# Windowed attention, low-rank mixer and MLP: all engines in one planned order, the mixer per head pair, exp then mask, and the mixer term added inside PSUM

## The chip, the cores and the metric

The kernel runs on one core of one Trainium2 chip. The metric is the device time of one execution in microseconds (us), median over several runs; lower is better. A profile is one execution recorded by the hardware profiler; its span runs from the first to the last instruction. PE is the matmul of TensorE, PEld its weight load, DVE is VectorE, ACT ScalarE, POOL GpSimd. "Fast" and "slow" are the two states that runs are sorted into; only fast runs are compared.

## The reference, cut to what matters

```python
# q, k, v: (4 batches, 8 heads, 768 positions, 64) in fp32; 8 global keys, a window of 96 keys
scores = q @ k.T / 8 - slope[h] * dist          # dist: distance, or 96 for a global key out of the window
scores = where(is_global | is_local, scores, -1e9)
a = softmax(scores);  x = a @ v                  # x: (4, 768, 512) after joining the heads
h = (x.T @ U @ V).T                              # U: (768, 32), V: (32, 768): mixes positions
u = x + h
out = u + relu(u @ w_ch1) @ w_ch2                # 512 -> 2048 -> 512
```

## The kernel before

Positions come in six blocks of 128, so a query block needs its own key block, the one before it, and the 8 global keys. Keys lie on the partitions of the score tiles. The parts that the argument touches:

```python
# loads: one transfer for each head, and for q, k and v; source runs of 64 fp32 = 256 B
nc.gpsimd.dma_start(stg[:, :, hi], src[b, h0 + hi].rearrange("(n p) d -> p n d", p=P))

# scores of a head: VectorE scales them out of PSUM and adds the bias, ScalarE takes exp
nc.vector.scalar_tensor_tensor(out=sprime[hi][:, soff:soff + tot], in0=sc[:, 0:tot],
    scalar=isl, in1=relcat[:, soff:soff + tot], op0=ALU.mult, op1=ALU.add)
nc.scalar.activation(epT[hi][:, 0:GOFF], sprime[hi], AF.Exp, scale=slope[h])

def mixer(b):                                    # a whole batch at once
    nc.scalar.activation(x16, xb, AF.Copy)       # 128 x 3072
    ... tmp = U.T x (6 matmuls of N=512), then for each of 6 token blocks:
        nc.tensor.matmul(h_ps, v16w[:, st * P:(st + 1) * P], tmp16, start=True, stop=True)
        nc.vector.tensor_tensor(xb[:, st], xb[:, st], h_ps, ALU.add)
    ... 24 transposes of fp32 x+h on TensorE, 8 copies to fp16 uT

# MLP in chunks of 512 tokens, held as a queue of small jobs
nc.tensor.matmul(hps, w1_16[:, dc, jt * P:(jt + 1) * P], uT[:, dc, tslice], ...)   # N=512
nc.scalar.activation(htr[:, jt], hps, AF.Relu)
nc.tensor.matmul(cps, htr[:, jc, tt * P:(tt + 1) * P], w2_16[:, jc], ...)           # N=512
nc.vector.tensor_tensor(osb, cps, x_sb[:, n], ALU.add)

for i, (b, hp) in enumerate(pairs):              # the order, by hand
    attention_pair(b, hp, loads.pop(0), fill)    # fill() puts MLP jobs between attention steps
    ...
    fill(3)
    if hp == 0 and b >= 1:
        mixer(b - 1)                             # after the first pair of the next batch
        ...
```

The softmax here doesn't subtract the row's maximum and nothing guards it: scores larger than these inputs give would overflow.

## Time and profile before

| | before |
|---|---|
| time, median of 4 runs | 339.56 us (338.38 to 340.17) |
| span of the profiled run | 341.3 us |
| first hidden-layer matmul (`hps`) starts | 74.2 us |
| TensorE idle from there to its end at 337.4 us | 263.2 - 244.0 = 19.2 us |

The first lines of the profile page. The first line gives busy time, share of the span and number of instructions for each engine; the rows below show the busy tenths of 40 slices of the span (PEclk: the granted clock of TensorE; DMA: the 16 DMA engines).

```profile
PE 288.9 (85%) x1808; PEld 137.7 (40%) x1808; DVE 148.9 (44%) x328; ACT 128.7 (38%) x165; POOL 93.7 (27%) x128
...
PE   0576745899879997998889899968999999999995
...
PEclk9999999999996999899999989998999999999999
DMA  6999999817991932386993307300200020011011
...
DMA packets 82452, 20.31 MB, mean 59 GB/s; under 512 B 76768, under 2 KB 78848, under 8 KB 82432
```

The same by stage. Columns of each row: the stretch and its length, busy time and instructions of each engine, granted clock, DMA share, GB/s.

```profile
core 0: us, PE busy (x) PEld busy (x) DVE busy (x) ACT busy (x) POOL busy (x), PEclk, DMA share, GB/s
0.00:74.20 74.20, 44.89 (x317) 24.71 (x318) 40.76 (x108) 23.02 (x22) 49.42 (x74) 1.00 1.25 114
74.20:240.00 165.80, 146.60 (x1038) 68.86 (x1037) 89.61 (x191) 77.03 (x95) 44.32 (x54) 0.95 0.55 47
240.00:341.30 101.30, 97.36 (x456) 44.12 (x454) 18.54 (x30) 28.68 (x48) 0.00 (x0) 1.00 0.10 39
```

TensorE is the bound in the third stage and nearly so in the second; in the first, 22% of the time, it is busy 60% and waits for others. Part of what it waits for at the end of that stage is the mixer of batch 0. The chain of waits between 54 and 75 us (start, length, what) shows it as one line of dependent work, 18.5 us from the cast to the first hidden-layer matmul:

```profile
55.78 2.77 ACT x_703 L262
...
58.59 2.73 PE tmp_ps L266 x6
...
62.08 0.58 PE h_ps L275
...
67.94 1.31 PE tpu L285 x5
...
70.05 4.27 PE tpu L285 x19
74.33 0.86 PE hps L307 x4
```

The groups of TensorE instructions (count | busy us, mean ns of one). A mean is no spacing, because the records of successive matmuls overlap: the mean is 386 ns, but the last 64 hidden-layer matmuls took 13.81 us by the chain of waits, which is 216 ns each.

```profile
L307 PE MATMUL hps<-uT,w_16_135 128*128 128x512 f16 x384 | 96.7, 386 | 0.3 <-DVE qT_1888 L186 0.3
L319 PE MATMUL cps<-w_16_136,htr 128*128 128x512 f16 x384 | 87.4, 382 | 0.1
...
L285 PE MATMUL tpu<-ident,x_sb 128*128 128x128 f32 x96 | 18.8, 360 | 1.9 <-DVE x_sb L278 1.8
```

### The profile page before, as it was taken

Reading aid. Unit: us, or ns where it says so; the run is one execution under the profiler, and the core shown is the slowest. Engines: PE = TensorE matmul, PEld = TensorE weight load, DVE = VectorE, ACT = ScalarE, POOL = GpSimd, SP = SyncE. Lnnn points to the kernel's source line nnn. Section 1 sums busy time; section 2 is a strip of 40 time slices with the busy share of each in tenths; the row PEclk is TensorE's granted clock in tenths of the full one; section 3 lists DMA queues with packets and bytes.
Section 4 is the critical chain, followed back from the end, with each engine's and each line's share of the span. In section 5 each row is a group of like instructions: output and inputs, shape, how many; then the busy total and the mean of one; then the engine's idle time right before and its main releaser. Section 6 shows DMA issues by size and latency. Waiting matters only on the chain.

```text
span 341.3 us, 4492 instructions
## 1 busy us (share of the span) xinstructions
PE 288.9 (85%) x1808; PEld 137.7 (40%) x1808; DVE 148.9 (44%) x328; ACT 128.7 (38%) x165; POOL 93.7 (27%) x128
## 2 busy tenths in 40 slices
PE   0576745899879997998889899968999999999995
PEld 0244322373333343643344363334354444444442
DVE  3564835565653537755553485662290010020011
ACT  1044444215456610276464016665006305504700
POOL 9966867204452310342350003100000000000000
PEclk9999999999996999899999989998999999999999
DMA  6999999817991932386993307300200020011011
GB/s 41 117 131 144 121 178 138 115 7 48 69 70 11 92 74 43 23 56 40 69 71 73 73 2 46 25 1 2 92 0 31 2 92 31 2 61 62 2 61 61
DMA packets 82452, 20.31 MB, mean 59 GB/s; under 512 B 76768, under 2 KB 78848, under 8 KB 82432
## 3 DMA queue, kind: packets, MB, share of 16 engines
q0 software_dynamic: 78976, 13.74, 51.6%
q1 hardware_dynamic: 3456, 6.29, 4.8%
q8 instruction: 14, 0.23, 0.3%
q14 instruction: 6, 0.05, 0.1%
HBM read 27.46 MB, written 6.29 MB: 99 GB/s over the span
## 4 chain that ended last, share of the span: by engine, by line
PE 66%; DVE 13%; ACT 8%; issue 7%; POOL 4%; DMA 1%; DVEq 0%; ACTq 0%; POOLq 0%
PE cps L319 25%; PE hps L307 21%; PE tpu L285 5%; PE sc L217 5%; PE ob L249 4%; DVE x_sb L278 2%; DVE x_sb L257 2%; POOL qkst L156 2%; PE tmp_ps L266 2%; PE tp L178 2%; PE sc L205 1%; PE h_ps L275 1%; DMA qkst<-in_k_dram 1%; ACT x_703 L262 1%; DVE rcp L254 1%
## 5 line engine op out<-in xcount | busy, mean ns | idle before, releaser
L311 ACT ACTIVATE htr<-hps 128x512 f16<-128x512 f32 x96 | 56.6, 597 | 147.7 <-PE hps L307 147.7
L307 PE MATMUL hps<-uT,w_16_135 128*128 128x512 f16 x384 | 96.7, 386 | 0.3 <-DVE qT_1888 L186 0.3
L319 PE MATMUL cps<-w_16_136,htr 128*128 128x512 f16 x384 | 87.4, 382 | 0.1
L319 PEld LDWEIGHTS <-htr 128*128 128x128 f16 x384 | 36.8, 98 | 48.2 <-issue 7.1
L324 DVE TENSOR_TENSOR osb<-cps,x_sb 128x512 f32<-128x512 f32 x24 | 16.6, 691 | 89.5 <-PE cps L319 89.3
L307 PEld LDWEIGHTS <-w_16_135 128*128 128x128 f16 x384 | 33.6, 98 | 42.7 <-issue 12.2
L156 POOL DMA_DIRECT2D qkst<-in_q_dram x32 | 26.8, 852 | 74.4 <-PE tp L178 74.0
L178 PE MATMUL tp<-ident_93,qkst 128*128 128x128 f16 x192 | 18.8, 249 | 12.9 <-DMA qkst<-in_q_dram 10.2
L156 POOL DMA_DIRECT2D qkst<-in_k_dram x32 | 28.0, 894 | 0.0
L178 PEld LDWEIGHTS <-qkst 128*128 128x128 f16 x192 | 14.4, 111 | 20.1 <-issue 14.2
L285 PE MATMUL tpu<-ident,x_sb 128*128 128x128 f32 x96 | 18.8, 360 | 1.9 <-DVE x_sb L278 1.8
L285 PEld LDWEIGHTS tpu<-ident,x_sb 128*128 128x128 f32 x96 | 15.5, 188 | 7.8 <-DVE x_sb L278 4.4
L257 DVE TENSOR_TENSOR x_sb<-ob,rcp 128x384 f32<-128x384 f32 x32 | 17.7, 554 | 2.0 <-DVE sprime_625 L225 1.4
L294 DVE CAST uT<-tpu 128x384 f16<-128x384 f32 x32 | 16.8, 554 | 1.7 <-PE tpu L285 0.4
L278 DVE TENSOR_TENSOR x_sb<-x_sb,h_ps 128x512 f32<-128x512 f32 x24 | 15.0, 680 | 3.7 <-PE h_ps L275 2.8
L254 DVE RECIPROCAL rcp<-ob 128x6 f32<-128x6 f32 x32 | 6.2, 193 | 12.5 <-PE ob L249 12.4
L145 POOL DMA_DIRECT2D w_16_136<-in_moe_w_ch_dram x16 | 8.6, 562 | 4.0 <-DMA w_16_135<-in_moe_w_ch_dram 3.6
L217 PE MATMUL sc<-qT_607,kT_608 64*128 64x256 f16 (+1 forms) x12 | 2.6, 384 | 4.5 <-DVE kT_608 L186 3.6
L208 ACT ACTIVATE epT_207<-sc,gcol 128x512 f16<-128x512 f32 x1 | 0.7, 687 | 15.0 <-PE sc L205 15.0
L275 PEld LDWEIGHTS <-v16w 32*128 32x128 f16 x24 | 2.1, 96 | 8.4 <-issue 7.6
L217 PE MATMUL sc<-qT_397,kT_398 64*128 64x256 f16 (+1 forms) x12 | 2.6, 389 | 2.5 <-DVE kT_398 L186 2.3
L262 ACT ACTIVATE x_703<-x_sb 128x3072 f16<-128x3072 f32 x1 | 2.8, 2763 | 4.3 <-DVE x_sb L257 4.3
(356 smaller groups left out, 313.8 us busy)
## 6 DMA issues: line engine op xcount, KB each, us to landing
out_dram<-osb SPq DMA_DIRECT2D x24, 256.0 KB, 2.0
qkst<-in_q_dram POOLq DMA_DIRECT2D x32, 96.0 KB, 3.3
qkst<-in_k_dram POOLq DMA_DIRECT2D x32, 96.0 KB, 3.5
w_16_135<-in_moe_w_ch_dram POOLq DMA_DIRECT2D x4, 512.0 KB, 7.7
w_16_136<-in_moe_w_ch_dram POOLq DMA_DIRECT2D x16, 128.0 KB, 5.6
v_145<-in_v_dram POOLq DMA_DIRECT2D x1, 96.0 KB, 3.3
v_148<-in_v_dram POOLq DMA_DIRECT2D x1, 96.0 KB, 3.4
v_157<-in_v_dram POOLq DMA_DIRECT2D x1, 96.0 KB, 3.4
```

Source lines behind the costliest of these rows:

```text
L156: nc.gpsimd.dma_start(stg[:, :, hi], src[b, h0 + hi].rearrange("(n p) d -> p n d", p=P),)
L178: nc.tensor.matmul(tp[:, sb * P:(sb + 1) * P], stg[:, sb].rearrange("s h d -> s (h d)"), ident16, is_transpose=True, start=(sb == 0), stop ...
L217: nc.tensor.matmul(sc[:, off:off + w], kTh[:, kb * P:(kb + 1) * P], qTh[:, kb * P:kb * P + w], start=(off == 0), stop=(off + w == tot),)
L249: nc.tensor.matmul(ob[:, qi], epT[hi][:, coff:coff + P], vt[:, kb], start=(bi == 0), stop=(bi == len(blks) - 1),)
L257: nc.vector.tensor_tensor(xo, ob[:, :, 0:D], rcpb, ALU.mult)
L278: nc.vector.tensor_tensor(xb[:, st], xb[:, st], h_ps, ALU.add)
L285: nc.tensor.matmul(tpu[:, ii * P:(ii + 1) * P], xb[:, st, dc * P:(dc + 1) * P], ident, is_transpose=True, start=(ii == 0), stop=(ii == 2),)
L294: nc.vector.tensor_copy(uT[:, dc, t0:t0 + 3 * P], tpu[:, 0:3 * P])
L307: nc.tensor.matmul(hps, w1_16[:, dc, jt * P:(jt + 1) * P], uT[:, dc, tslice], start=(dc == 0), stop=(dc == NDC - 1),)
L311: nc.scalar.activation(htr[:, jt], hps, AF.Relu)
L319: nc.tensor.matmul(cps, htr[:, jc, tt * P:(tt + 1) * P], w2_16[:, jc], start=(jc == 0), stop=(jc == NJC - 1),)
L324: nc.vector.tensor_tensor(osb, cps, x_sb[:, n], ALU.add)
```

## The change

The intent: let no engine wait for another by accident of program order. A small planner inside the kernel knows every task (engine, duration, what it depends on, which buffer it takes), simulates the engines, and gives one program order for all. With it go four changes of arithmetic and layout: q and k of two heads in one transfer with 1536 B runs; exp straight from PSUM, then one fp16 multiply with a ready mask; the mixer per head pair, on fp16 transposes, with x and h summed by TensorE in PSUM; the MLP by whole batch (N=384 halves), with the mixer term of the output as one more matmul of the same accumulation.

```diff
+            if t.size:                                   # Planner.run: a load
+                begin = max(t.end + 1.6, dma_free)
+                t.end = begin + t.size / self.dma_rate
... (the rest of the planner is cut)
-                    src[b, h0 + hi].rearrange("(n p) d -> p n d", p=P),
+                    dst[gs.slot], src[b, h0:h0 + 2].rearrange("h (p n) d -> p h (n d)", n=NB)
...
-                    nc.vector.scalar_tensor_tensor(
-                        out=sprime[hi][:, soff:soff + tot], in0=sc[:, 0:tot],
-                        scalar=isl, in1=relcat[:, soff:soff + tot],
-                        op0=ALU.mult, op1=ALU.add,
-                    )
+                nc.scalar.activation(
+                    ep[gep.slot][:, :, lo:512], psum(gsc)[:, :, lo:512], AF.Exp, scale=qk_scale
+                )
+                    nc.vector.tensor_tensor(ev, ev, mv, ALU.mult)
...                                                       # shifted copies, on VectorE and GpSimd
+            nc.gpsimd.tensor_copy(vof, vv[:, :, 0:NB - 1])
...                                                       # mixer of a pair: x.T by identity, + V.T tmp
+                        t[:, half, ii * P:(ii + 1) * P], xx[:, 3 * half + ii], ident16,
+                        start=(ii == 0), stop=False, skip_group_check=True,
+                    psum(gx)[:, half, 0:HS], tmp[b % 2][:, hp * P:(hp + 1) * P],
+                    vrep[:, half * HS:(half + 1) * HS], start=False, stop=True, skip_group_check=True,
...                                                       # output: two token tiles in one PSUM tile
+            g = Group("mlp", readers=2)
+            for kk in range(2):
+                        o = psum(g)[:, kk]
+                        if lo == 0:
+                            nc.tensor.matmul(o, vrep[:, tt * P:(tt + 1) * P], tb, start=True, stop=False)
+                        for jc in range(lo, hi_):
+                            nc.tensor.matmul(o, hb[:, jc, tt * P:(tt + 1) * P], w2[:, jc], ...)
+                    nc.vector.tensor_tensor(osb[go.slot], psum(g)[:, kk], xb[:, tt], ALU.add)
...
+    order = pl.run()
+    with tc.manual_schedule():
+        for t in order:
+            t.fn()
```

## The prediction

> **What bounds the kernel now.** The busy table puts TensorE at 288.9 of 341.3 us (85%); VectorE has 44%, ScalarE 38%, GpSimd 27%. Three stages:
> 1. 0 to 74 us (timeline: first hidden-layer matmul at 74.3 us): not TensorE. GpSimd issues half-head loads one by one (0.82 to 0.89 us each) and the DMA row is near full: 76,768 of 82,452 packets are under 512 B. TensorE runs cold: N=256 score matmuls take 400 ns here, 273 later.
> 2. 74 to 240 us: attention of batches 1 to 3 mixed with the MLP. The windows show TensorE idle about 20 us, mostly behind VectorE's score-bias pass (0.69 us a chunk); the granted clock dips to 0.8 in places, worth some 8 us.
> 3. 240 us to the end: matmul at its limit, 64 of N=512 in 13.81 us, 216 ns each.
>
> **What the change does.**
> - Loads: q and k of two heads in one transfer with 1536 B source runs instead of 256 B; v stays. Packets fall from ~79,000 to ~37,000, q/k/v issues from 192 to 48. The Trainium skill, "DMA: Bandwidth & Descriptors", Specifications, puts line rate at 512 B and more; the near-full DMA row agrees.
> - Attention: score-bias pass and long exp (1.37 us) are replaced by exp straight from PSUM and an fp16 mask multiply. Estimates per head pair: ScalarE 4.7 us, VectorE 5 to 6, GpSimd 5: under 95 us each in all, off the path once the MLP runs.
> - MLP: 512 matmuls of N=384 (estimate 216x384/512 = 162 ns) = 83 us and 408 of N=512 (one more per token tile for the mixer term) = 88 us: 171 us against 166. No gain here.
> - Mixer: fp32 transposes (24 in 4.61 us), VectorE's x+h pass and the 2.76 us cast of each batch go; fp16 transposes and three small matmul groups per pair come.
> - TensorE attention and mixer per pair at warm rates of the trace (transposes 63 ns, PV about 35, N=128 scores about 40 with the two heads overlapping): 1.4 + 0.85 + 0.8 + 1.05 = about 4.1 us.
> - Each switch of tile shape between MLP and attention costs about 0.1 us (score pairs between hidden-layer matmuls show it).
>
> **On the critical path.** TensorE's own work hardly falls (about 245 to 237 us). The gain is start and idle time.
> - Start: first transposes at 5 us instead of 7.9, four pairs at 6 to 7 us each (TensorE cold, DMA 6 us a pair), plus the pair pipeline's depth of 12 us: MLP at about 35 us instead of 74.
> - Then 171 + 12 x 4.1 = 220 us of TensorE, 8 us of switches, 5 us of stalls or clock dips, a tail of 3 us (add 0.7, store 2.0).
>
> **Predicted: 270 us, 8 in 10 between 253 and 289.** Faster by over 2%: 0.97; within 2%: 0.02; slower: 0.01.
>
> **What would show it.** First hidden-layer matmul at 30 to 42 us; TensorE over 93% busy from there; its waits on VectorE under 5 us in the middle; under 40,000 packets; VectorE and ScalarE below 45%; the last 40 us solid MLP at 216 ns per N=512 and 162 per N=384.
>
> **What would make it wrong.** The in-order plan uses fixed durations: if mask multiplies, GpSimd copies or DMA land later than planned, TensorE stalls at the head of its queue and nothing overtakes (280 to 300). VectorE's multiplies and GpSimd's copies may slow each other. Weight loads of N=384 matmuls may not hide. If head pairs overlap fully in the array, TensorE work falls to 225 and the time to 255.

## The result, and the profile after

| | before | after |
|---|---|---|
| time, median of 4 runs | 339.56 us | 270.69 us (270.47 to 271.06) |
| ratio | | 0.7976, 95% interval 0.7952 to 0.7999 |
| span of the profiled run | 341.3 us | 268.7 us |
| first hidden-layer matmul | 74.2 us | 36.4 us |
| from there to the end of the last output matmul | 263.2 us | 228.4 us |

A ratio is the mean time of one kernel's fast runs over that of the other's of the same rounds, so it is not quite the ratio of the medians. The spans differ by 72.6 us, somewhat more than the medians (68.9 us), because the profiled run of before was a little longer than its timed runs. Those 72.6 us are 74.2 - 36.4 = 37.8 us of start and 263.2 - 228.4 = 34.8 us after it.

The page of the changed kernel, the lines that answer to those of before:

```profile
PE 241.3 (90%) x2232; PEld 136.9 (51%) x2232; DVE 103.5 (39%) x190; ACT 122.3 (46%) x157; POOL 84.4 (31%) x118
...
PE   1568697999999999999999898999999989998893
...
PEclk9985569999999999999999999999999999999998
DMA  7994999996932577439428112000011220001122
...
DMA packets 42214, 20.74 MB, mean 77 GB/s; under 512 B 26704, under 2 KB 38992, under 8 KB 42192
```

By stage (start; overlap of attention and MLP; the last batch's MLP alone):

```profile
core 0: us, PE busy (x) PEld busy (x) DVE busy (x) ACT busy (x) POOL busy (x), PEclk, DMA share, GB/s
0.00:36.40 36.40, 21.78 (x306) 15.97 (x307) 21.69 (x39) 20.85 (x29) 31.26 (x52) 0.75 1.09 138
36.40:219.00 182.60, 176.17 (x1701) 98.64 (x1699) 76.96 (x145) 88.46 (x112) 53.18 (x66) 0.99 0.52 76
219.00:268.70 49.70, 43.35 (x231) 22.30 (x228) 4.84 (x7) 12.96 (x16) 0.00 (x0) 0.98 0.10 38
```

In the start GpSimd is busy 31.26 of 36.4 us and TensorE works at three quarters of its clock. The overlap is as full as one could ask, 96% of TensorE. The last stage is odd: nothing is left there but matmuls, and TensorE is busy only 43.35 of 49.7 us. The timeline from 240 us (start, length, engine, line) shows why:

```profile
239.90 3.62 PE L585 MATMUL ps<-w,htr 128*128 128x512 f16 x16
...
243.57 1.89 PE L585 MATMUL ps<-w,htr 128*128 128x512 f16 x8
245.56 0.69 DVE L603 TENSOR_TENSOR osb<-ps,x_sb 128x512 f32<-128x512 f32 x1 [25.78 <-PE ps L585]
...
246.30 1.89 PE L585 MATMUL ps<-w,htr 128*128 128x512 f16 x8 [0.84 <-DVE osb L603]
```

Token tile 0 is finished at about 243.5 us, but its add starts only after eight matmuls of tile 1, and the other eight of tile 1 wait for the add. Both tiles lie in one PSUM tile (its two banks). The trace puts this wait of 0.84 us down to the add. No data asks for it. The kernel has twelve such pairs of token tiles. In six of them the wait stands open in the trace (0.78 to 0.84 us each, 4.8 us in all); in the other six, other matmuls stand between the two halves or the add is done in time.

The TensorE groups after:

```profile
L585 PE MATMUL ps<-w,htr 128*128 128x512 f16 x384 | 89.6, 379 | 4.8 <-DVE osb L603 4.8
L551 PE MATMUL ps<-uT,w 128*128 128x384 f16 x512 | 92.3, 329 | 1.0 <-ACT htr L568 0.6
```

By the chain of waits the last 128 hidden-layer matmuls took 20.80 us (162.5 ns each) and 16 output matmuls 3.45 us (216 ns each).

### The profile page after: what moved, and what is told of

It reads as the page before. It is cut to its first block, busy times and chain, and to the rows that moved or that the text cites. A ratio compares the mean times of both kernels' runs of the same rounds, so it can differ in the third digit from the quotient of the medians.

```text
span 268.7 us, 5138 instructions
## 1 busy us (share of the span) xinstructions
PE 241.3 (90%) x2232; PEld 136.9 (51%) x2232; DVE 103.5 (39%) x190; ACT 122.3 (46%) x157; POOL 84.4 (31%) x118
## 2 busy tenths in 40 slices
DMA packets 42214, 20.74 MB, mean 77 GB/s; under 512 B 26704, under 2 KB 38992, under 8 KB 42192
## 4 chain that ended last, share of the span: by engine, by line
PE 83%; POOL 5%; DVE 5%; DMA 4%; issue 1%; ACT 0%; DVEq 0%; POOLq 0%
PE ps L551 32%; PE ps L585 31%; PE ps L398 4%; DMA vt<-in_v_dram 4%; PE ps L338 3%; PE ps L502 3%; DVE osb L603 3%; PE ps L583 2%; PE ps L443 2%; PE ps L510 2%; PE ps L442 2%; PE ps L486 1%; POOL stgk L281 1%; POOL vo L374 1%; POOL w L300 1%
## 5 line engine op out<-in xcount | busy, mean ns | idle before, releaser
L585 PE MATMUL ps<-w,htr 128*128 128x512 f16 x384 | 89.6, 379 | 4.8 <-DVE osb L603 4.8
L551 PE MATMUL ps<-uT,w 128*128 128x384 f16 x512 | 92.3, 329 | 1.0 <-ACT htr L568 0.6
L568 ACT ACTIVATE htr<-ps 128x768 f16<-128x768 f32 x64 | 51.6, 811 | 47.2 <-PE ps L551 46.8
L551 PEld LDWEIGHTS <-w 128*128 128x128 f16 x512 | 47.2, 98 | 32.1 <-issue 2.1
L585 PEld LDWEIGHTS <-htr 128*128 128x128 f16 x384 | 36.8, 98 | 48.3 <-issue 7.3
L409 ACT ACTIVATE ep<-ps 128x1024 f16<-128x1024 f32 (+1 forms) x48 | 44.7, 953 | 33.9 <-PE ps L398 33.9
L603 DVE TENSOR_TENSOR osb<-ps,x_sb 128x512 f32<-128x512 f32 x24 | 16.6, 691 | 74.3 <-PE ps L585 74.2
L422 DVE TENSOR_TENSOR ep<-ep,mask 128x1024 f16<-128x1024 f16 x32 | 27.5, 860 | 21.9 <-ACT ep L409 21.9
L443 PE MATMUL ps<-vt,ep 128*128 128x65 f16 x192 | 19.1, 204 | 0.1
L442 PE MATMUL ps<-vo,ep 128*128 128x65 f16 x160 | 17.4, 204 | 1.7 <-DVE ep L422 1.7
L398 PE MATMUL ps<-qT,kT 64*128 64x128 f16 x192 | 17.1, 236 | 1.6 <-ACT qT L351 1.6
L443 PEld LDWEIGHTS <-ep 128*128 128x128 f16 x192 | 15.3, 104 | 4.2 <-issue 0.7
L442 PEld LDWEIGHTS <-ep 128*128 128x128 f16 x160 | 13.5, 105 | 4.5 <-DVE ep L422 2.5
```

The lines of the kernel that those rows point to most:

```text
L398: nc.tensor.matmul(t[:, hi, j * P:(j + 1) * P], lhs, qt[r, i * P:(i + 1) * P], start=True, stop=True,)
L409: nc.scalar.activation(ep[gep.slot][:, :, lo:512], psum(gsc)[:, :, lo:512], AF.Exp, scale=qk_scale)
L422: nc.vector.tensor_tensor(ev, ev, mv, ALU.mult)
L442: nc.tensor.matmul(o, e[:, hi, j * P:(j + 1) * P], vof[:, hi, i - 1], start=True, stop=False)
L443: nc.tensor.matmul(o, e[:, hi, (j + 1) * P:(j + 2) * P], vv[:, hi, i], start=(i == 0), stop=True)
L551: nc.tensor.matmul(t[:, half, 0:HS], w1[:, dc, jt * P:(jt + 1) * P], ub[:, dc, half * HS:(half + 1) * HS], start=(dc == 0), stop=(dc == ND ...
```

## The experiments

Every experiment is one edit of the changed kernel, whose time is 270.69 us; times are medians of 4 fast runs. The kernel before, run beside them, had its fast runs at 338.8 to 342.5 us in the first two calls and at 341.8 to 346.5 us in the third (combined versions, serial, no mixer term), so times of different calls are compared with that much care. "Start" is the first hidden-layer matmul (36.4 us in the changed kernel).

| run | edit | time | against 270.69 | start |
|---|---|---|---|---|
| e1_alternate | output tiles in different PSUM tiles | 262.50 | -8.2 | 36.6 |
| e6_poolfree | no batch-0 copies on GpSimd | 266.56 | -4.1 | 34.0 |
| e2_loads256 | 256 B runs for q, k | 273.51 | +2.8 | 38.5 |
| e5_warm | batch-0 transposes and scores twice | 271.26 | +0.6 | 36.8 |
| e3_bias | VectorE bias pass and late exp | 276.93 | +6.2 | 43.9 |
| e11_latemix | mixer after the whole batch | 281.83 | +11.1 | 53.0 |
| e9_fp32x | fp32 transposes of x | 285.61 | +14.9 | 38.0 |
| e7_flatplan | plan with all durations 1.0 us | 310.75 | +40.1 | 54.7 |
| e8_serial | no overlap of batches | 350.69 | +80.0 | 36.9 |
| e4_noterm | mixer term left out of the output | 264.87 | -5.8 | 37.3 |
| c1_both | e1 and e6 | 259.73 | -11.0 | 36.7 |
| c2_measured | c1, plan with measured durations | 257.46 | -13.2 | 33.5 |

All results were correct but that of e4_noterm.

### e1_alternate: is the wait for the output add real?

```diff
-            g = Group("mlp", readers=2)
             for kk in range(2):
+                g = Group("mlp", readers=1)
                 tt = 2 * t2 + kk
-                        o = psum(g)[:, kk]
+                        o = psum(g)[:, 0]
-                    nc.vector.tensor_tensor(osb[go.slot], psum(g)[:, kk], xb[:, tt], ALU.add)
+                    nc.vector.tensor_tensor(osb[go.slot], psum(g)[:, 0], xb[:, tt], ALU.add)
```

> One edit to the changed kernel: neighbouring token tiles of the output matmul go to different PSUM tiles in turn, instead of to the two banks of one. Theory A: in the changed kernel the second half of every second token tile waits for the VectorE add of the first one only because both lie in one PSUM tile; that is 12 stops of about 0.84 us with nothing to overtake, so the time falls by 7 to 10 us, to 261 to 264 us, and the TensorE waits for the output add vanish. Theory B: TensorE would be held by something else there (weight loads, clock), so the wait moves and the time changes by less than 2 us.

Measured 262.50 us, 8.2 us less. The timeline of the last batch now runs through; the add overlaps the next tile:

```profile
238.44 3.62 PE L585 MATMUL ps<-w,htr 128*128 128x512 f16 x16
238.49 0.69 DVE L603 TENSOR_TENSOR osb<-ps,x_sb 128x512 f32<-128x512 f32 x1 [23.83 <-PE ps L585]
...
242.11 3.62 PE L585 MATMUL ps<-w,htr 128*128 128x512 f16 x16
```

The time is in the range of theory A, and no TensorE wait for the output add is left. The count behind the range was wrong, though: not twelve stops stood open but six. An open stop costs more than its 0.84 us of idle time: in the last batch a pair of token tiles took 8.34 us before (239.69 to 248.03) and 7.34 us now (234.56 to 241.90). Six stops of 1.0 us, two short waits for the add (0.6 us together) and one mask multiply that queued on VectorE behind such an add (TensorE waited 1.1 us for it at 151 us) come to 7.7 of the 8.2 us, as an estimate from these numbers. In e8_serial, where attention does not fill the gaps, all twelve stand open:

```profile
PE ps L585 <- DVE osb L603: 9.9, 12, 0.9
```

### e6_poolfree: what bounds the start?

The shifted copy of v, the cast of x and the casts of U and V move to VectorE in batch 0:

```diff
-            nc.gpsimd.tensor_copy(vof, vv[:, :, 0:NB - 1])
+            ve = nc.vector if vo_eng == DVE else nc.gpsimd      # DVE for p < NP
+            ve.tensor_copy(vof, vv[:, :, 0:NB - 1])
-            (nc.vector if last else nc.gpsimd).tensor_copy(x16[gx16.slot], src)
+            (nc.vector if xc_dve else nc.gpsimd).tensor_copy(x16[gx16.slot], src)
```

> For the four head pairs of batch 0 the shifted copy of v and the fp16 cast of x go from GpSimd to VectorE, with the casts of U and V. Theory A: GpSimd's in-order queue (95% busy up to 30 us) bounds the start, so the first hidden-layer matmul moves from 36.4 us to 29 to 33 us and the time falls by 3.5 to 7 us. Theory B: the cold TensorE or the DMA bounds the start: first hidden-layer matmul at 35 to 37 us, time within 1.5 us. If VectorE becomes the bound instead, the start is later than 37 us.

Measured 266.56 us, 4.1 us less, with the start at 34.0 us: the time is in the range of theory A, the start a little short of it. GpSimd's queue held the start by 2.4 us; the rest was won after it. A second effect shows in the mask multiplies of VectorE. These are the fastest, median and slowest of them, first in the changed kernel:

```profile
L422 DVE TENSOR_TENSOR ep<-ep,mask x32: 678/693/2755, 13.1 to 189.0; 128x1024 f16<-128x1024 f16 x32
```

and with the copies moved:

```profile
L425 DVE TENSOR_TENSOR ep<-ep,mask x32: 670/692/1274, 15.5 to 184.1; 128x1024 f16<-128x1024 f16 x32
```

The two multiplies around the slow one span 19.3 to 23.2 us, while GpSimd does casts and copies back to back. The Trainium skill, "GPSIMD Engine Reference", Specifications, says that GpSimd's SBUF interfaces are shared with VectorE and that they contend with VectorE instructions of two SBUF inputs, which these are. The trace agrees, with 2.76 us for a multiply that takes 0.69 us otherwise. That the shared interface is the cause was not isolated.

### e2_loads256: do the wide loads make the start?

```diff
-                    dst[gs.slot], src[b, h0:h0 + 2].rearrange("h (p n) d -> p h (n d)", n=NB)
+                    dst[gs.slot].rearrange("p h (n d) -> p h n d", n=NB),
+                    src[b, h0:h0 + 2].rearrange("h (n p) d -> p h n d", p=P),
```

(and the copies out of the transposes keep the plain order)

> Only the load layout of q and k is undone: still one transfer for two heads, but with 256 B source runs as before the change; all else, the plan too, stays. Theory A: packets rise from 42,000 to about 67,000, the DMA engines become the bound of the first batch (about 10 us a pair at the rate of before), first hidden-layer matmul at 45 to 58 us, time 280 to 291 us. Theory B: the start is bound by the engines and not by packets: time up by less than 4 us.

Measured 273.51 us, 2.8 us more, and the start moved by 2.1 us, although the packets doubled:

```profile
DMA packets 83174, 20.74 MB, mean 76 GB/s; under 512 B 75856, under 2 KB 79952, under 8 KB 83152
```

Theory A falls. The kernel with as many small packets as before starts its MLP at 38.5 us and not at 74. The near-full DMA row of before was a fact, but small packets alone were not the bound. The edit keeps two heads in one transfer; the other half of the load change, 48 issues for q, k and v instead of 96, was not undone.

### e5_warm: does the cold clock bound the start?

```diff
-            for which, stg in ((0, stgq[gs.slot]), (1, stgk[gs.slot])):
+            for which, stg in ((0, stgq[gs.slot]), (1, stgk[gs.slot])) * (2 if p < NP else 1):
-                for j in range(4):
+                for j in list(range(4)) * (2 if p < NP else 1):
```

> The transposes and score matmuls of batch 0 are done twice (same result) to keep TensorE busier and its clock granted from 18 to 38 us. Theory A: TensorE's cold clock is not the bound of the start, GpSimd's queue is: time within -2 to +4 us, whether the clock comes up or not. Theory B: the cold clock bounds it: clock near 1.0 from 18 us on and the time down by 3 to 6 us.

Measured 271.26 us, within theory A. The clock did come up. The stretch from 18 us to the start of the MLP, first of the changed kernel (the column after the POOL count is the clock):

```profile
18.00:36.40 18.40, 14.32 (x176) 10.02 (x176) 15.04 (x25) 11.06 (x15) 15.12 (x20) 0.50 0.98 141
```

and with the doubled work:

```profile
18.00:37.00 19.00, 13.67 (x311) 10.77 (x306) 14.11 (x27) 12.22 (x17) 16.12 (x20) 0.93 0.92 131
```

The clock went from 0.50 to 0.93, the start stayed at 36.8 us. The matmuls confirm it: twelve transposes took 0.53 us at 21 us instead of 0.85 us at 20 us. The last pair's mixer stayed cold, however: its six U matmuls at 34.2 us took 0.40 us, as in the changed kernel. The Trainium skill, "TensorE: Matmul & The Clock Gate", Part 1, describes half rate as the state of a matmul engine that was too little busy; the value of 0.50 here agrees. So up to 34 us the cold clock does not set the pace of this start. This does not rule out that a warm clock alone, without the doubled work, or in the last pair too, would have won a little. The changed kernel's own runs point the same way: mean clocks of 0.959 and 0.993 gave 270.51 and 270.47 us. But the column alone can mislead: for the kernel before it reads 1.00 in the first 74 us, where an N=256 score matmul took 400 ns against 273 ns later. The durations of like matmuls decide.

### e3_bias: was the VectorE score pass the brake?

```diff
-                nc.scalar.activation(ep[...], psum(gsc)[...], AF.Exp, scale=qk_scale)   # both heads
-                    nc.vector.tensor_tensor(ev, ev, mv, ALU.mult)
+                        nc.vector.scalar_tensor_tensor(out=..., in0=t..., scalar=isl,   # each head
+                            in1=rel3..., op0=ALU.mult, op1=ALU.add)
+                    nc.scalar.activation(e, e, AF.Exp, scale=slope[h0 + hi])
```

> The old arithmetic is put back into the planned order: VectorE scales the scores out of PSUM and adds the bias, ScalarE takes exp of the fp16 result, one instruction per head (the plan is told the longer durations). Theory A: VectorE and ScalarE are off the path once the MLP runs, so only the four pairs of the start pay: first hidden-layer matmul 4 to 8 us later than 36.4 us, time 275 to 281 us. Theory B: the VectorE score pass is what held TensorE in the middle of the old kernel and holds it again: time above 290 us.

Measured 276.93 us, 6.2 us more, with the start 7.5 us later. Theory A by its numbers: in the middle VectorE's load went up (125.4 us busy in all instead of 103.5) without a further loss. But most of the later start is not the score pass itself. TensorE's longest wait before the MLP is for a cast of x on GpSimd:

```profile
PE ps L481 <- POOL x L470: 10.4, 2, 7.8
```

The x that it casts was ready at 34.3 us (VectorE, L455), and the cast began at 40.4 us. In between GpSimd's queue stood at load issues, which waited in their turn:

```profile
34.63 0.72 POOL L271 DMA_DIRECT2D stgk<-in_k_dram  x1 [1.82 <-DMA w<-in_moe_w_ch_dram]
37.40 1.04 POOL L277 DMA_DIRECT2D vt<-in_v_dram  x1 [2.05 <-DMA w<-in_moe_w_ch_dram]
...
40.42 0.83 POOL L470 CAST x<-x_sb 128x768 f16<-128x768 f32 x1
```

So about 6 of the 7.5 us come from where this plan put one cast. With the cast in time, the score pass would cost the start some 1.5 us (an estimate from these numbers; no run isolates it).

### e11_latemix: is the mixer per pair worth it?

The tasks of the mixer are the same, but each depends on the last pair's attention of its batch (`NM = nm_of[b * NP + NP - 1]`) and they are added after the batch.

> The mixer of every pair (cast, U product, transposes, V product, copies) starts only when the attention of the whole batch is done, as in the old kernel; the instructions are the same. Theory A: doing the mixer per pair hides its chain behind the next pairs' attention; undone, the first hidden-layer matmul comes 4 to 9 us later, the middle is unchanged, time 275 to 280 us. Theory B: the last pair's chain set the start anyway: time within 1.5 us of 270.7.

Measured 281.83 us, 11.1 us more; the start moved by 16.6 us. Both are larger than expected. Of the 17 us from 36 to 53 us TensorE was busy 6.2 us, 10 us of it in one wait, for a cast of x in GpSimd's queue:

```profile
PE ps L496 <- POOL x L485: 10.0, 1, 10.0
```

The cause is the one of e3: the x of batch 0 was complete at 34.2 us (VectorE), and the first cast on GpSimd began at 44.8 us, behind load issues. Without that the start would come some 7 us later, which is what was expected (an estimate: 16.6 less the 10 us). So this run does not show that waiting for the whole batch costs 16.6 us; it shows that plus a badly placed cast. Part of the later start is won back afterwards, because attention of batch 1 had gone ahead.

### e9_fp32x: what do the fp16 transposes save?

```diff
-                        t[:, half, ii * P:(ii + 1) * P], xx[:, 3 * half + ii], ident16,   # x16
+                        t[:, half, ii * P:(ii + 1) * P], xx[:, 3 * half + ii], ident,     # x_sb, fp32
```

(the plan is told 0.6 us for three instead of 0.18)

> The identity matmuls that transpose x read the fp32 x again instead of its fp16 cast. Theory A: TensorE is the bound after the start, so 72 to 96 of them at about 0.19 us instead of 0.06 us (0.03 to 0.06 in the new trace) lengthen the time by 9 to 13 us, to 280 to 284 us. Theory B: they hide in TensorE's waits: under 4 us.

Measured 285.61 us, 14.9 us more, 1.6 us of it in the start. Theory A, even a little above its range: each of these matmuls is on the path, since TensorE is the bound after the start; its busy time rose by 15.9 us (257.2 instead of 241.3).

### e7_flatplan: how much hangs on the order?

```diff
-        t = pl.add(eng, dur, prio, fn, deps, **kw)
+        t = pl.add(eng, 1.0 if eng != SP else dur, prio, fn, deps, **kw)
```

> Same instructions, but the planner is told that every compute task lasts 1.0 us, so that its order is no longer fitted to the chip. Theory A: the fitted order is worth something but not most of the gain: 276 to 286 us, with more waits of TensorE in the middle. Theory B: the fitted order is the gain: above 295 us. Theory C: any order that overlaps batches will do: within 2 us of 270.7.

Measured 310.75 us, 40.1 us more with the same instructions, above 295 us as theory B had it: 18.3 us in the start, the rest after it. Its costliest TensorE waits (total, times, longest):

```profile
PE ps L486 <- POOL x L475: 21.7, 6, 7.9
...
PE ps L338 <- DMA stgq<-in_q_dram: 8.2, 2, 5.8
```

A cast that the bad plan put behind other work on GpSimd stops TensorE for up to 7.9 us, and nothing behind it can overtake. This shows that an order unfit for the chip costs more than half of the change's gain. It does not show that a hand-made order of the new instructions would be as bad.

### e8_serial: what is the overlap worth?

```diff
-        T = add(PE, 1.2, base, tr, [tq, tk, c_id16], ...)
+        T = add(PE, 1.2, base, tr, [tq, tk, c_id16] + ([osb_done[b - 1]] if b else []), ...)
```

> The attention of a batch may start only when the output of the batch before is done: no overlap between attention and MLP, all else as in the changed kernel. Theory A: overlap hides nearly the whole latency of three batches of attention; without it each costs 15 to 28 us more than its TensorE work, time 315 to 355 us. Theory B: attention is TensorE work anyway: below 300 us.

Measured 350.69 us, 80.0 us more, 26.7 us for each of three batches. All gain is gone. Two rows of its page show that the attention stretches are also cold:

```profile
PE   1685699998667859999957786999985757799994
...
PEclk9956889999955568999985556999997557899999
```

Overlap hides the latency of attention and keeps the clock up at once; the runs do not part the two.

### e4_noterm: the price of the mixer term in the output

```diff
-                        if lo == 0:
-                            nc.tensor.matmul(o, vrep[:, tt * P:(tt + 1) * P], tb, start=True, stop=False)
```

> Wrong result on purpose: the mixer term's matmul is left out of the output accumulation (24 matmuls of N=512). Theory A: TensorE is the bound, the 24 matmuls cost their 24 x 216 ns = 5.2 us: 265 to 266.5 us. Theory B: they hide in the waits around the output add: less than 2 us.

Measured 264.87 us, 5.8 us less, against 24 x 216 ns = 5.2 us: theory A, just under its range. It is a new price: before, 24 matmuls of N=512 made h once (`h_ps`); now 32 of N=384 (L510) make it for the hidden layer, and these 24 make it again for the output. What it buys is that VectorE's add of h (15.0 us busy) goes.

### c1_both and c2_measured: the best version

c1_both holds the edits of e1 and e6. c2_measured adds the trace's durations:

```diff
-        T = add(PE, 1.2, ...                     +        T = add(PE, 0.8, ...
-        tq = add(POOL, 0.5, ...                  +        tq = add(POOL, 0.7, ...        # tk alike
-        tv = add(POOL, 1.7, ..., size=0.39e6     +        tv = add(POOL, 1.04, ..., size=0.8e6
-                begin = max(t.end + 1.6, dma_free)
+                begin = max(t.end + 2.5, dma_free)
```

(and small corrections of the exp and the v copy)

> The two edits that helped, together: alternating PSUM tiles in the output matmul (8.2 us alone) and no batch-0 copies on GpSimd (4.1 us alone). Theory A: they act in different stages and add up: 257.5 to 260 us. Theory B: the earlier start is eaten by the middle: 261 to 263 us.

> The combined version with the planner told the durations that the trace of the changed kernel shows (transposes 0.8 us instead of 1.2, load issues 0.7 and 1.04 us, a later landing of loads). Theory A: the order is sensitive to durations only when they are far off; within 2 us of the combined version. Theory B: a truer plan removes more waits: 3 us or more below it.

c1_both took 259.73 us (258.00 to 260.26), within the range of theory A: 8.2 + 4.1 = 12.3 us expected, 11.0 got. Its reason is not shown. The earlier start of e6 (34.0 us) is not there: c1 starts at 36.7 us, and by 60 us it had issued 88 hidden-layer matmuls, as e1 alone did (86), and not 98 as e6 alone did. What c1 wins over e1, it wins later. c2_measured took 257.46 us (256.62 to 258.42), 2.3 us below it. That lies between the two theories, and the ranges of the two touch, so whether a truer plan helps beyond c1 stays open. Against the changed kernel c2_measured is 13.2 us faster (4.9%), in a call in which the kernel before was slower, not faster, than elsewhere. It beats both kernels.

## Why the prediction was right

The predicted time, 270 us, is the measured one (270.69). The sum behind it is less good than it looks; taken point by point:

1. **Start at about 35 us: right (36.4), but for a wrong reason.** The prediction put the wide loads first and the cold clock and 6 us of DMA for each pair into the sum. e2 gives the length of the load runs 2.1 us of the start, and e5 found no gain in a warmer clock. Undoing the mixer per pair moved the start by 16.6 us (e11) and undoing the score pass by 7.5 us (e3); but some 10 and 6 us of these are a cast of x that the plans of those runs put behind load issues on GpSimd. So what made the start short is open for the larger part of the 37.8 us. Untried candidates are that before ran a fifth pair ahead of its first mixer, and the halved number of load issues. GpSimd's queue still holds the start a little (2.4 us in e6, not seen in c1).
2. **TensorE work of a pair, 4.1 us: too much.** Counted from the trace as the time from each matmul's start to the next one's, idle time left out, the matmuls of attention and mixer take 42.5 us between 36.4 us and the end of the output matmuls: about 3.5 us for each of 12 pairs, where the prediction had 49 us. The mis-sized term is the transposes, put at 1.4 us for a pair and measured at 0.78 (48 in 1.56 us). They go to two halves of the array's columns in turn and take 32 ns each instead of 63; the Trainium skill, "TensorE: Matmul & The Clock Gate", Part 3, describes such tiles working at once, and the trace agrees. The same count gives the MLP's matmuls 176.6 us instead of 171.3; the difference of 5.3 us holds the switches, put at 8.
3. **Stalls and clock dips 5 us, "the last 40 us solid MLP": wrong.** TensorE's recorded idle time after 36.4 us is 8.9 us, and 5.4 of it are waits for the output add; with what hangs on them they cost 8.2 us (e1). They were not foreseen. They were in the diff: two token tiles in one PSUM tile. The prediction looked for waits of VectorE's load and found that small; this wait comes from how a tile is shared. Terms 2 and 3 pull in opposite directions: 49 + 8 + 5 = 62 us foreseen, 42.5 + 5.3 + 8.9 = 56.7 us measured. That the total fits to 1 us is partly luck: its parts are off by 3 to 7 us, in both directions.
4. **MLP 171 us, 162 ns for N=384, 216 ns for N=512, no gain there: right.** 162.5 and 216 ns; e4 confirms the price of the extra matmul.
5. **fp16 transposes for fp32 on TensorE: right in direction, small in the text.** "TensorE's own work hardly falls" hid that this part alone is worth 14.9 us (e9).
6. **The order: named as a risk, not as a gain.** TensorE is busy 94% from the start of the MLP on (over 93% foreseen), and e7 and e8 show what that hangs on: 40 us with a bad plan, 80 us without overlap. The warning that nothing overtakes at the head of a queue is what e7 shows.
7. **Small checks.** Packets 42,214 instead of under 40,000; ScalarE 46% instead of under 45%; VectorE 39%: the first two just missed. First transposes at 5.95 us instead of 5. The issues for q, k and v were 96 before (32 each in the trace), not 192, and are 48 now; they were whole heads. TensorE's recorded waits for VectorE's add alone come to 5.4 us, more than the 5 us foreseen.

Undoing costs do not sum to the gain (2.8 + 6.2 + 11.1 + 14.9 = 35.0 of 68.9 us). What single parts cost when undone need not add up, and the rest was not isolated; the order and the fewer waits that go with it are the likely place.

## What to carry to other kernels

Check a full-looking resource by doubling its load before building on it: the DMA row was full, and doubling the packets cost 2.8 us. Where an in-order program is the plan, look for buffers that two independent results share, since a wait there stops everything behind it: alternating two tiles won 8.2 us. And keep work that feeds the bottleneck off any queue that also has to wait for something else: in e3, e7 and e11 one cast of x behind load issues on GpSimd stopped TensorE for 7.8 to 10 us.

## What the Trainium skill lacked or had wrong

- "TensorE: Matmul & The Clock Gate", Back-to-back issue gap, gives about 131 ns for each N=512 matmul in a stream of weight loads and matmuls and says that N/2.4 + 2.5 ns over-counts there. Here such streams take 216 ns each (16 in 3.45 us; 64 in 13.81 us before), with a weight load for every matmul, and N=384 takes 162.5 ns (128 in 20.80 us): the formula holds and the 131 ns do not.
- "DMA: Bandwidth & Descriptors", Specifications, ties line rate to 512 B. Here, 75,856 instead of 26,704 packets under 512 B cost 2.8 us of 271, though the DMA row is near full in the start. The page does not say that a full row need not be the bound.
- "GPSIMD Engine Reference", Specifications, names the contention with VectorE but gives no size there (how long the blocked side waits stands on another page of the skill): a mask multiply of 0.69 us took up to 2.76 us beside GpSimd copies, and a 128x40 copy of 0.16 us up to 0.79 us.
- No page that was read says that the wait between two results in different banks of one PSUM tile can come from how the tile is tracked and not from the data: six open stops of about 0.8 us in the trace, 8.2 us in all by e1.
